# A decode step on one core: a split request for w_down and unrolled ScalarE copies, in place of hardware loops and a short ScalarE program

## The chip, the core and the metric

The kernel runs on one core of a Trainium2 chip. The metric is the device time of one execution in microseconds (us). A core has five engines that run their own programs and meet at semaphores: TensorE (PE; its weight loads are listed as PEld), VectorE (DVE), ScalarE (ACT), GpSimd (POOL) and SyncE (SP), which issues most of the DMA requests. Sixteen DMA engines move the data; a request over 128 partitions arrives in sixteen shares, one from each, and its semaphore counts to 16.

## What is computed

One token goes through two branches in parallel, each fed by the same layer norm, and both are added to the input:

```python
xn = layernorm(x)                                  # x: 1 x 512, bf16
# branch A: sliding-window attention on a cache
q = xn @ wq                                        # 512 x 4096: 32 heads of 128
k, v = k_cache[:, :, -4096:], v_cache[:, :, -4096:]   # 8 key heads, 4 query heads each
o = softmax(q @ k.T * 128**-0.5) @ v
a = o @ wo                                         # 4096 x 512
# branch B: a gated MLP for the one token
r = xn @ w_r                                       # one token: top-1 is this token
y = (silu(xn @ w_gate) * (xn @ w_up)) @ w_down     # 512 x 1792, 1792 x 512
b = xn + sigmoid(r) * y
out = x + a + b
```

wq and wo have 4 MB each, the windows of k and v 8 MB each, w_gate, w_up and w_down 1.75 MB each. In all 30.7 MB are read once, for a single output row of 1 KB.

## The kernel before

All work is written out by hand: each engine has its own order, and `need` waits for a token that another engine's `mark` counts up, while the loops use plain semaphores. Nothing plans or reorders it.

*Requests.* SyncE asks for everything in one order: wq in two chunks (kt 0-1, kt 2-3), w_r (1 KB), the eight 1 MB groups of k, the eight of v, then, when the q projection is done, w_gate and w_up into the space of wq, and, when the last half of group 5 has been staged (`SP.need((s_c[1], 6))`, L326), wo in four chunks of 1 MB and w_down in five chunks (of 4, 4, 3, 2 and 1 of its 14 row blocks) into the space of k. Only x is asked for by ScalarE. Each request has its own semaphore.

*Norm and q.* VectorE and ScalarE normalize x (Sqrt, L181). TensorE turns the row into four columns (L190) and multiplies them with wq, in two passes kh = 0, 1 over the two chunks (L223); each pass fills two PSUM banks (hf). Between the passes stand the gate and two matmuls that zero the score banks: VectorE multiplies xn with w_r (L202), ScalarE takes Tanh (L205), VectorE scales (L207), TensorE spreads the value over the partitions (L214), VectorE copies it (gfb, L216). The two banks of q are copied by ScalarE and by VectorE (L230), and transposed into qpad (L236, L240).

*K loop.* For each of the eight groups g, VectorE copies k into a staging tile kin in two halves of 2048 columns (C, L265). TensorE transposes four blocks b of 8 x 128 columns into PSUM (T, L296). The evacuation to kT goes to VectorE for b = 0, 2 (E, L269) and to ScalarE for b = 1, 3, in a hardware loop (L283 to L286). TensorE multiplies with the queries (Sm, L304), the second pair of blocks one round late, so that its order in a round is T0 T1, S2 S3 of the group before, T2 T3, S0 S1. GpSimd copies the queries of a group to qA and qB (L256, L258).

*Softmax and V loop.* Row maxima (L335 to L349), Exp on ScalarE (L351), transposes of p (L360). Then for each group VectorE stages v in two halves and picks the columns of p (L369, L373, L375), TensorE multiplies (L402, L408) and collects the four bands (L393) of the group before, which ScalarE has copied from PSUM to pvS in a second hardware loop (L386 to L388).

*The end.* The gate and up products (L433), the normalized attention output in the layout of wo (L438, L440), then 32 matmuls with the four chunks of wo (L456) and 14 with the five of w_down (L461), all into one PSUM row; VectorE adds the input (L465) and SyncE stores it. `fill` (L146) issues matmuls on zeros, whose result nobody reads, while TensorE would otherwise stand still.

Of the kernel before, what the change touches and what calls it, by code (L numbers as in the profile page):

```python
# [8 lines left out]
F32 = mybir.dt.float32  # L9
ALU = mybir.AluOpType  # L10
ACTF = mybir.ActivationFunctionType
# [27 lines left out]
def kernel(  # L39
# [15 lines left out]
    P = 128  # L55
    D = A_x.shape[2]
    KT = D // P
    HKV = A_k_cache.shape[1]
# [18 lines left out]
    sb = lambda name, shape, dt: nc.alloc_sbuf_tensor(name, shape, dt)  # L77
    k_sb = sb("k_sb", [P, HKV, 4, 1024], BF16)
    v_sb = sb("v_sb", [P, HKV, NT, DH], BF16)
    wq_sb = sb("wq_sb", [P, KT, NQ], BF16)  # L80
    kin = sb("kin", [P, 4, 1024], BF16)
    kT = sb("kT", [P, 4, 1024], BF16)
# [7 lines left out]
    q4 = sb("q4", [P, 2, 512], BF16)  # L90
# [3 lines left out]
    gfb = sb("gfb", [P, 1], F32)  # L94
    ident_bf = sb("ident_bf", [P, P], BF16)
    ident_f = sb("ident_f", [P, P], F32)
    ones_f = sb("ones_f", [P, P], F32)
# [2 lines left out]
    mask4 = sb("mask4", [P, 4], BF16)  # L100
    r32 = sb("r32", [P, 32], BF16)
    eps_t = sb("eps_t", [P, 1], F32)
    xrow = sb("xrow", [1, D], BF16)
    wr_row = sb("wr_row", [1, D], BF16)
    xn_row = sb("xn_row", [1, D], BF16)
# [5 lines left out]
    sml = sb("sml", [1, 8], F32)  # L111
# [12 lines left out]
    ps = nc.alloc_psum_tensor("ps", [P, 8, 512], F32)  # L124
    psf = ps[:].rearrange("p a b -> p (a b)")
    tp = ps[:, 0:4, :].bitcast(BF16)
# [9 lines left out]
    wd_sb = k_flat[:, 0:FB * D]  # L136
    wo_sb = k_flat[:, FB * D:(FB + RJ) * D]

    S = lambda n: nc.alloc_semaphore(n)
    PE, ACT, DVE, POOL, SP = (Eng(nc, nc.tensor, "pe"), Eng(nc, nc.scalar, "act"), Eng(nc, nc.vector, "dve"),  # L140
                              Eng(nc, nc.gpsimd, "pool"), Eng(nc, nc.sync, "sp"))
    te, ac, ve, gp, sy = nc.tensor, nc.scalar, nc.vector, nc.gpsimd, nc.sync
# [5 lines left out]
    def dma(eng, name, out_, in_):  # L148
        s = S("d_" + name)
        eng.dma_start(out=out_, in_=in_).then_inc(s, 16)  # L150
        return (s, 16)

    t_x = dma(ac, "x", xrow[:], A_x.rearrange("a b d -> (a b) d"))
    wq_v = A_wq.rearrange("(p kt) n -> p kt n", kt=KT)
    KH = KT // 2
    t_wq = [dma(sy, f"wq{h}", wq_sb[:, h * KH:(h + 1) * KH, :], wq_v[:, h * KH:(h + 1) * KH, :]) for h in range(2)]
    t_wr = dma(sy, "wr", wr_row[:], B_w_r.rearrange("(a d) -> a d", a=1))
    t_k = [dma(sy, f"k{g}", k_sb[:, g].rearrange("p b (i d) -> p (b i) d", d=DH),
               A_k_cache[0, g, Sk - W:, :].rearrange("(p t) d -> p t d", t=NT)) for g in range(HKV)]

# [11 lines left out]
    t_eps = DVE.mark(ve.memset(eps_t[:], EPS))  # L172
    t_ones = DVE.mark(ve.memset(ones_f[:], 1.0))
    t_ps0 = DVE.mark(ve.memset(ps[:, 0:2, :].rearrange("p a b -> p (a b)"), 0.0))

    DVE.need(t_x)
    a = DVE.mark(ve.bn_stats(out=stats[:], in_=xrow[:]))
    DVE.need(a)
    t_mv = DVE.mark(ve.bn_aggr(out=mv[:], in_=stats[:]))
    ACT.need(t_mv, t_eps)  # L180
    t_std = ACT.mark(ac.activation(out=sml[:, 0:1], in_=mv[:, 1:2], func=ACTF.Sqrt, bias=eps_t[0:1, :], scale=1.0))  # L181
    DVE.need(t_std)
    a = DVE.mark(ve.reciprocal(out=sml[:, 1:2], in_=sml[:, 0:1]))
    DVE.need(a, t_mv)
# [4 lines left out]
    for kt in range(KT):  # L189
        ins = te.matmul(ps[:, 6, 256 + kt:257 + kt], lhsT=xn_row[:].rearrange("a (p k) -> a k p", k=KT)[:, kt, :],  # L190
                        rhs=ident_bf[0:1, 0:1], start=True, stop=True)
# [13 lines left out]
    t_rth = ACT.mark(ac.activation(out=sml[:, 3:4], in_=sml[:, 2:3], func=ACTF.Tanh, scale=0.5))  # L205
    DVE.need(t_rth)
    t_gf = DVE.mark(ve.tensor_scalar(out=sml[:, 4:5], in0=sml[:, 3:4], scalar1=0.25, scalar2=0.25, op0=ALU.mult, op1=ALU.add))  # L207
    PE.need(t_xnT)
    t_qe = []
    t_qpad = []  # L210
    for kh in range(2):
        if kh == 1:
            PE.need(t_gf, t_ones)
            t_gfp = PE.mark(te.matmul(ps[:, 6, 264:265], lhsT=ones_f[0:1, :], rhs=sml[:, 4:5], start=True, stop=True))  # L214
            DVE.need(t_gfp)
            t_gfb = DVE.mark(ve.tensor_copy(out=gfb[:], in_=ps[:, 6, 264:265]))  # L216
            for ch in range(2):
                te.matmul(sc[:, ch, :], lhsT=zst[:], rhs=zmov[:], start=True, stop=False, skip_group_check=True)  # L218
        PE.need(t_wq[kh], t_ps0)
        for hf in range(2):  # L220
            for kt in range(kh * KH, (kh + 1) * KH):
                for c in range(4):
                    ins = te.matmul(ps[32 * c:32 * c + 1, hf, :], lhsT=xnT[:, kt:kt + 1],  # L223
                                    rhs=wq_sb[:, kt, (4 * hf + c) * 512:(4 * hf + c + 1) * 512],
                                    start=(kt == 0), stop=(kt == KT - 1), tile_position=(0, 32 * c))
            if kh == 1:
                t_qp = PE.mark(ins)
                cp, eng = ((ac.copy, ACT), (ve.tensor_copy, DVE))[hf]
                eng.need(t_qp)
                t_qe.append(eng.mark(cp(out=q4[:, hf, :], in_=ps[:, hf, :])))  # L230
    for hf in range(2):
        PE.need(t_qe[hf], t_gfb)
        if hf == 1:
# [1 line left out]
        for hl in range(4):  # L235
            ins = te.transpose(qT_ps[:, hl, :], q4[:, hf, hl * DH:(hl + 1) * DH], ident_bf[:])  # L236
# [7 lines left out]
    t_g = dma(sy, "g", wgu[:, 0:KT * F], B_w_gate.rearrange("(p kt) f -> p (kt f)", kt=KT))  # L244
    t_u = dma(sy, "u", wgu[:, KT * F:2 * KT * F], B_w_up.rearrange("(p kt) f -> p (kt f)", kt=KT))

    s_c = [S(f"s_c{b}") for b in range(2)]
    s_ev = [S(f"s_ev{b}") for b in range(4)]
    pe_t = [S(f"pe_t{b}") for b in range(4)]
    pe_q = S("pe_q")  # L250

    def pool_q(g):
        POOL.need(t_qpad[g // 4])
# [3 lines left out]
        gp.wait_ge(pe_q, 2 * g + 1)  # L257
        gp.tensor_copy(out=qB[:], in_=qpad[:, g, :]).then_inc(s_qb, 1)  # L258

    def C(g, h):  # L260
        if h == 0:
            DVE.need(t_k[g])
        if g >= 1:
            DVE.need((pe_t[2 * h + 1], g))
        ve.tensor_copy(out=kin[:, 2 * h:2 * h + 2, :], in_=k_sb[:, g, 2 * h:2 * h + 2, :]).then_inc(s_c[h], 1)  # L265

    def E(g, b):
        DVE.need((pe_t[b], g + 1))
        ve.tensor_copy(out=kT[:, b, :], in_=tp[:, b, :]).then_inc(s_ev[b], 1)  # L269

    for h in range(2):
        C(0, h)
    for g in range(HKV):
        pool_q(g)
        last = (g == HKV - 1)
        E(g, 0)
        if not last:
            C(g + 1, 0)
        E(g, 2)
        if not last:  # L280
            C(g + 1, 1)

    with ac.Fori(1, 9) as i:  # L283
        for b in (1, 3):
            ac.wait_ge(pe_t[b], i)
            ac.copy(out=kT[:, b, :], in_=tp[:, b, :]).then_inc(s_ev[b], 1)  # L286

    PE.need(t_zst, t_zmov, t_kt0)
    te.sem_inc(s_ev[2], 1)
    te.sem_inc(s_ev[3], 1)  # L290

    def T(b, i):
        if b % 2 == 0:
            te.wait_ge(s_c[b // 2], i)
        for k in range(8):
            ins = te.transpose(tp[:, b, k * P:(k + 1) * P], kin[:, b, k * P:(k + 1) * P], ident_bf[:])  # L296
        ins.then_inc(pe_t[b], 1)

    def Sm(b, i, q, last=False):
        te.wait_ge(s_ev[b], i)  # L300
# [10 lines left out]
    with te.Fori(1, 9) as i:  # L311
# [11 lines left out]
    Sm(2, 9, qB)  # L323
    t_sc = PE.mark(Sm(3, 9, qB))

    SP.need((s_c[1], 6))  # L326
    wo_v = A_wo.rearrange("(p j) n -> p (j n)", j=RJ)
    wo_chunks = [(0, 8), (8, 16), (16, 24), (24, 32)]
    t_wo = [dma(sy, f"wo{k}", wo_sb[:, j0 * D:j1 * D], wo_v[:, j0 * D:j1 * D]) for k, (j0, j1) in enumerate(wo_chunks)]
    wd_v = B_w_down.rearrange("(p j) n -> p (j n)", j=FB)  # L330
    wd_chunks = [(0, 4), (4, 8), (8, 11), (11, 13), (13, 14)]
    t_wd = [dma(sy, f"wd{k}", wd_sb[:, j0 * D:j1 * D], wd_v[:, j0 * D:j1 * D]) for k, (j0, j1) in enumerate(wd_chunks)]

    DVE.need(t_sc)
    t_pmax = DVE.mark(ve.reduce_max(out=pmax[:], in_=sc[:].rearrange("p a b -> p (a b)"), axis=AX.X))  # L335
# [4 lines left out]
    a = DVE.mark(ve.reduce_max(out=gm[:], in_=ps[0:1, 6, 0:P].rearrange("a (q c) -> a c q", q=4), axis=AX.X))  # L340
# [6 lines left out]
                              start=True, stop=True))  # L347
# [8 lines left out]
    for h in range(2):  # L356
        PE.need(t_p[h])
        for k in range(4):
            blk = 4 * h + k
            ins = te.transpose(pT_ps[:, blk, :], p_sb[:, blk * P:(blk + 1) * P], ident_bf[:])  # L360
    t_pT = PE.mark(ins)

    s_va, s_vb, s_pt, pe_pva, pe_pv, s_pvs, pe_col = S("s_va"), S("s_vb"), S("s_pt"), S("pe_pva"), S("pe_pv"), S("s_pvs"), S("pe_col")

    def stage_v(g):
        DVE.need(t_v[g])
        if g >= 1:
            DVE.need((pe_pva, g))
        ve.tensor_copy(out=vin[:, 0], in_=v_sb[:, g, 0:16, :]).then_inc(s_va, 1)  # L369
        DVE.need(t_pT)  # L370
        if g >= 1:
            DVE.need((pe_pv, g))
        ve.tensor_copy(out=pTcur[:].rearrange("p b (q j) -> p b q j", j=REP),  # L373
                       in_=pT_ps.rearrange("p b (q c) -> p b q c", q=4)[:, :, :, REP * g:REP * (g + 1)]).then_inc(s_pt, 1)
        ve.tensor_copy(out=vin[:, 1], in_=v_sb[:, g, 16:32, :]).then_inc(s_vb, 1)  # L375
# [4 lines left out]
    a = DVE.mark(ve.tensor_tensor(out=rs1[:], in0=rowsum[:, 0:1], in1=rowsum[:, 1:2], op=ALU.add))  # L380
    DVE.need(a, t_r32)
    t_B = DVE.mark(ve.tensor_scalar(out=Bsel[:], in0=r32[:], scalar1=rs1[:], scalar2=None, op0=ALU.mult))

    for g in range(1, HKV):
        stage_v(g)
    with ac.Fori(1, 9) as i:  # L386
        ac.wait_ge(pe_col, i)
        ac.copy(out=pvS[:].rearrange("p t d -> p (t d)"), in_=pv_ps).then_inc(s_pvs, 1)  # L388
    PE.need(t_pv0)

# [5 lines left out]
    with te.Fori(1, 9) as i:  # L396
        g = i - 1
# [3 lines left out]
        for tl in range(4):  # L401
            ins = te.matmul(pv_ps[32 * tl:32 * tl + 16, :], lhsT=pTcur[:, tl, :],  # L402
                            rhs=vin[:, 0].rearrange("p (q t) d -> p t q d", t=4)[:, tl],
                            start=True, stop=False, tile_position=(0, 32 * tl))
        ins.then_inc(pe_pva, 1)
        te.wait_ge(s_vb, i)
        for tl in range(4):
            ins = te.matmul(pv_ps[32 * tl:32 * tl + 16, :], lhsT=pTcur[:, 4 + tl, :],  # L408
                            rhs=vin[:, 1].rearrange("p (q t) d -> p t q d", t=4)[:, tl],
                            start=False, stop=True, tile_position=(0, 32 * tl))  # L410
# [45 lines left out]
            te.matmul(a_ps, lhsT=oT2[:, j:j + 1], rhs=wo_sb[:, j * D:(j + 1) * D], start=False, stop=False, skip_group_check=True)  # L456
    PE.need(t_hT)
    for k, (j0, j1) in enumerate(wd_chunks):
        PE.need(t_wd[k])
        for j in range(j0, j1):  # L460
            ins = te.matmul(a_ps, lhsT=hTr[:, j, 0:1], rhs=wd_sb[:, j * D:(j + 1) * D], start=False, stop=(j == FB - 1),  # L461
                            skip_group_check=True)
# [36 lines left out]
```

## Time and profile before

| | |
|---|---|
| median of 3 runs | 82.53 us (82.31 to 82.58) |
| profiled execution | 82.31 us, of which the span from its first to its last instruction is 80.5 |
| busy: PE, DVE, ACT, POOL | 60.2, 45.1, 26.5, 10.6 us |
| HBM read | 30.67 MB, 381 GB/s over the span |
| q projection, second pass (L223) | from 15.64 us |
| K loop | 19.9 to 45.2 us |
| V loop | 50.4 to 64.1 us |
| wo and w_down (L456, L461) | 67.3 to 77.7 us |

A line such as `L456 PE MATMUL ps<-k_sb,oT` is the matmul of line 456 that writes tile ps from tiles k_sb and oT; wo and w_down lie in the space of k_sb and are listed under its name. A group's line ends with its busy time and the mean of one instruction, and with the idle time of the engine before it and what ended that. Digits in the slices are tenths. Matmul ends are modelled, and a matmul's duration contains its passage through the array, so the time from start to start says more on the rate. DMA packets and the arrival of each share of a request are also in the trace.

### The profile page before, as it was taken

How to read it: one execution, taken by the hardware profiler on the slowest of the kernel's cores; microseconds unless marked ns; L12 is line 12 of the kernel's file. 1: busy time of each engine (PE TensorE's matmuls, PEld its weight loads, DVE VectorE, ACT ScalarE, POOL GpSimd, SP SyncE). 2: the span in 40 equal slices, each digit the busy share in tenths (PEclk: the TensorE clock that was granted, in tenths of full speed). 3: DMA queues.
4: the chain of work that ended last, by engine and by line, in shares of the span. 5: the costliest groups of instructions: out<-in, count | busy, mean ns of one | idle time of the engine just before them, and what ended most of it. 6: DMA issues, size and time to landing. Idle time of an engine off the chain costs nothing.

```text
span 80.5 us, 1589 instructions
## 1 busy us (share of the span) xinstructions
PE 60.2 (75%) x596; PEld 30.7 (38%) x596; DVE 45.1 (56%) x91; ACT 26.5 (33%) x34; POOL 10.6 (13%) x27
## 2 busy tenths in 40 slices
PE   0010810993999999999999786788887899999950
PEld 0010200422787686868776232222222443333300
DVE  3771004026655999999995547988888059000030
ACT  2830001020135787777777216222343220000000
POOL 5910000001011253434341000000000000000000
PEclk9999999999999999999999999999999999999999
DMA  1999999999999999999999999999999999999400
GB/s 41 301 431 399 431 448 395 419 431 423 427 427 419 415 427 415 431 415 431 415 427 419 419 415 419 448 430 420 420 449 381 423 423 423 423 403 392 176 2 1
DMA packets 4185, 30.72 MB, mean 381 GB/s; under 512 B 467, under 2 KB 598, under 8 KB 1110
## 3 DMA queue, kind: packets, MB, share of 16 engines
q1 hardware_dynamic: 4180, 30.67, 92.0%
q8 instruction: 2, 0.03, 0.2%
q14 instruction: 1, 0.01, 0.0%
q10 hardware_dynamic: 2, 0.00, 0.0%
HBM read 30.67 MB, written 0.00 MB: 381 GB/s over the span
## 4 chain that ended last, share of the span: by engine, by line
PE 62%; DMA 14%; ACT 9%; DVE 7%; issue 4%; SPq 1%; ACTq 0%
PE ps L296 23%; DMA wr_row<-in_B_w_r_dram 14%; PE ps L456 9%; PE ps L304 7%; ACT pvS L388 6%; PE ps L461 4%; PE ps L402 3%; PE ps L408 3%; PE ps L393 2%; PE ps L223 2%; PE ps L433 2%; DVE pmax L335 2%; ACT kT L286 1%; PE ps L146 1%; PE ps L218 1%
## 5 line engine op out<-in xcount | busy, mean ns | idle before, releaser
L296 PE MATMUL ps<-ident_bf,kin 128*128 128x128 bf16 x256 | 19.4, 236 | 0.9 <-DVE kin L265 0.9
L286 ACT COPY kT<-ps 128x1024 bf16<-128x1024 bf16 x16 | 16.2, 1012 | 11.2 <-PE ps L296 11.2
L296 PEld LDWEIGHTS ps<-ident_bf,kin 128*128 128x128 bf16 x256 | 16.5, 106 | 5.0 <-issue 3.8
L269 DVE COPY kT<-ps 128x1024 bf16<-128x1024 bf16 x16 | 11.1, 692 | 3.3 <-PE ps L296 2.7
L265 DVE COPY kin<-k_sb 128x2048 bf16<-128x2048 bf16 x16 | 10.9, 686 | 0.5 <-PE ps L296 0.4
L388 ACT CAST pvS<-ps 128x512 bf16<-128x512 f32 x8 | 4.7, 585 | 9.6 <-PE ps L393 9.6
L456 PE MATMUL ps<-k_sb,oT 128*1 128x512 bf16 x32 | 7.2, 379 | 0.0
L223 PE MATMUL ps<-wq_sb,xnT 128*1 128x512 bf16 x32 | 3.8, 621 | 3.5 <-DMA wq_sb<-in_A_wq_dram 3.5
L256 POOL COPY qA<-qpad 128x32 bf16<-128x32 bf16 x8 | 3.6, 448 | 21.1 <-DVE qpad L240 14.1
L369 DVE COPY vin<-v_sb 128x2048 bf16<-128x2048 bf16 x8 | 5.5, 685 | 1.5 <-PE ps L402 1.5
L465 DVE TENSOR_TENSOR res<-ps,resid 1x512 bf16<-1x512 f32 x1 | 0.7, 678 | 9.1 <-PE ps L461 9.1
L375 DVE COPY vin<-v_sb 128x2048 bf16<-128x2048 bf16 x8 | 5.5, 684 | 0.0
L402 PE MATMUL ps<-vin,pTcur 128*16 128x512 bf16 x32 | 3.1, 381 | 2.6 <-ACT pvS L388 2.2
L258 POOL COPY qB<-qpad 128x32 bf16<-128x32 bf16 x8 | 3.6, 451 | 10.4 <-PE ps L304 10.4
L414 PE MATMUL ps<-zmov,zst 128*128 128x512 bf16 x16 | 4.7, 377 | 0.0
L304 PE MATMUL ps<-kT,qB 128*32 128x512 bf16 x36 | 4.2, 413 | 0.4 <-ACT kT L286 0.3
L202 DVE SCALAR_TENSOR_TENSOR rprod<-xn_row,wr_row 1x512 f32<-1x512 bf16 x1 | 0.7, 679 | 6.7 <-DMA wr_row<-in_B_w_r_dram 6.7
L456 PEld LDWEIGHTS ps<-k_sb,oT 128*1 128x1 bf16 x32 | 2.5, 84 | 4.6 <-DMA k_sb<-in_A_wo_dram 0.5
L190 PE MATMUL ps<-ident_bf,xn_row 1*128 1x1 bf16 x4 | 0.3, 166 | 4.6 <-DVE xn_row L185 4.6
L146 PE MATMUL ps<-zmov,zst 128*128 128x512 bf16 x14 | 3.7, 382 | 0.0
L214 PE MATMUL ps<-sml,ones_f 1*128 1x1 f32 x2 | 0.6, 358 | 3.9 <-DVE sml L207 3.9
L304 PE MATMUL ps<-kT,qA 128*32 128x512 bf16 x32 | 3.4, 417 | 0.0
(84 smaller groups left out, 51.3 us busy)
## 6 DMA issues: line engine op xcount, KB each, us to landing
k_sb<-in_A_k_cache_dram SPq DMA_DIRECT2D x8, 1024.0 KB, 20.5
v_sb<-in_A_v_cache_dram SPq DMA_DIRECT2D x8, 1024.0 KB, 27.3
wq_sb<-in_A_wq_dram SPq DMA_DIRECT2D x2, 2048.0 KB, 9.6
k_sb<-in_A_wo_dram SPq DMA_DIRECT2D x4, 1024.0 KB, 31.4
wq_sb<-in_B_w_gate_dram SPq DMA_DIRECT2D x1, 1792.0 KB, 29.0
wq_sb<-in_B_w_up_dram SPq DMA_DIRECT2D x1, 1792.0 KB, 31.2
k_sb<-in_B_w_down_dram SPq DMA_DIRECT2D x2, 512.0 KB, 29.6
k_sb<-in_B_w_down_dram SPq DMA_DIRECT2D x1, 384.0 KB, 25.7
```

The costliest lines, as they stand in the source:

```text
L223: ins = te.matmul(ps[32 * c:32 * c + 1, hf, :], lhsT=xnT[:, kt:kt + 1], rhs=wq_sb[:, kt, (4 * hf + c) * 512:(4 * hf + c + 1) * 512], start ...
L265: ve.tensor_copy(out=kin[:, 2 * h:2 * h + 2, :], in_=k_sb[:, g, 2 * h:2 * h + 2, :]).then_inc(s_c[h], 1)
L269: ve.tensor_copy(out=kT[:, b, :], in_=tp[:, b, :]).then_inc(s_ev[b], 1)
L286: ac.copy(out=kT[:, b, :], in_=tp[:, b, :]).then_inc(s_ev[b], 1)
L296: ins = te.transpose(tp[:, b, k * P:(k + 1) * P], kin[:, b, k * P:(k + 1) * P], ident_bf[:])
L304: ins = te.matmul(sc[32 * cq:32 * cq + 32, ch, :], lhsT=q[:], rhs=kT[:, b, e * 512:(e + 1) * 512], start=False, stop=False, tile_position= ...
L369: ve.tensor_copy(out=vin[:, 0], in_=v_sb[:, g, 0:16, :]).then_inc(s_va, 1)
L375: ve.tensor_copy(out=vin[:, 1], in_=v_sb[:, g, 16:32, :]).then_inc(s_vb, 1)
L388: ac.copy(out=pvS[:].rearrange("p t d -> p (t d)"), in_=pv_ps).then_inc(s_pvs, 1)
L402: ins = te.matmul(pv_ps[32 * tl:32 * tl + 16, :], lhsT=pTcur[:, tl, :], rhs=vin[:, 0].rearrange("p (q t) d -> p t q d", t=4)[:, tl], start ...
L414: te.matmul(ps[:, 7, :], lhsT=zst[:], rhs=zmov[:], start=True, stop=True)
L456: te.matmul(a_ps, lhsT=oT2[:, j:j + 1], rhs=wo_sb[:, j * D:(j + 1) * D], start=False, stop=False, skip_group_check=True)
```

## The change

- ScalarE's copies in the K and V loops are written out instead of looped over; its program has 50 instructions instead of 30.
- In the K loop ScalarE also evacuates block 0 of groups 1, 3 and 5. VectorE stages k in four copies of 1024 columns per group; the four transposes count on one semaphore, each staging copy on one of its own, and a staging copy waits for its own block's transpose.
- w_r is asked for by ScalarE, after x. The gate's matmul and copy (L214, L216) stand before both passes of the q projection. Both banks of q are copied by ScalarE.
- ScalarE runs a one-element Sqrt and a one-element Tanh whose results nobody reads.
- The first chunk of w_down is asked for in two requests: partitions 0 to 119 (15 DMA engines) and 120 to 127.

```diff
@@ -100,6 +100,7 @@
     mask4 = sb("mask4", [P, 4], BF16)
     r32 = sb("r32", [P, 32], BF16)
     eps_t = sb("eps_t", [P, 1], F32)
+    junk = sb("junk", [1, 2], F32)
     xrow = sb("xrow", [1, D], BF16)
     wr_row = sb("wr_row", [1, D], BF16)
     xn_row = sb("xn_row", [1, D], BF16)
@@ -151,10 +152,10 @@
         return (s, 16)
 
     t_x = dma(ac, "x", xrow[:], A_x.rearrange("a b d -> (a b) d"))
+    t_wr = dma(ac, "wr", wr_row[:], B_w_r.rearrange("(a d) -> a d", a=1))
     wq_v = A_wq.rearrange("(p kt) n -> p kt n", kt=KT)
     KH = KT // 2
     t_wq = [dma(sy, f"wq{h}", wq_sb[:, h * KH:(h + 1) * KH, :], wq_v[:, h * KH:(h + 1) * KH, :]) for h in range(2)]
-    t_wr = dma(sy, "wr", wr_row[:], B_w_r.rearrange("(a d) -> a d", a=1))
     t_k = [dma(sy, f"k{g}", k_sb[:, g].rearrange("p b (i d) -> p (b i) d", d=DH),
                A_k_cache[0, g, Sk - W:, :].rearrange("(p t) d -> p t d", t=NT)) for g in range(HKV)]
 
@@ -172,13 +173,16 @@
     t_eps = DVE.mark(ve.memset(eps_t[:], EPS))
     t_ones = DVE.mark(ve.memset(ones_f[:], 1.0))
     t_ps0 = DVE.mark(ve.memset(ps[:, 0:2, :].rearrange("p a b -> p (a b)"), 0.0))
+    ACT.need(t_eps)
+    ac.activation(out=junk[:, 0:1], in_=eps_t[0:1, :], func=ACTF.Sqrt)
 
     DVE.need(t_x)
     a = DVE.mark(ve.bn_stats(out=stats[:], in_=xrow[:]))
     DVE.need(a)
     t_mv = DVE.mark(ve.bn_aggr(out=mv[:], in_=stats[:]))
-    ACT.need(t_mv, t_eps)
+    ACT.need(t_mv)
     t_std = ACT.mark(ac.activation(out=sml[:, 0:1], in_=mv[:, 1:2], func=ACTF.Sqrt, bias=eps_t[0:1, :], scale=1.0))
+    ac.activation(out=junk[:, 1:2], in_=eps_t[0:1, :], func=ACTF.Tanh)
     DVE.need(t_std)
     a = DVE.mark(ve.reciprocal(out=sml[:, 1:2], in_=sml[:, 0:1]))
     DVE.need(a, t_mv)
@@ -205,15 +209,16 @@
     t_rth = ACT.mark(ac.activation(out=sml[:, 3:4], in_=sml[:, 2:3], func=ACTF.Tanh, scale=0.5))
     DVE.need(t_rth)
     t_gf = DVE.mark(ve.tensor_scalar(out=sml[:, 4:5], in0=sml[:, 3:4], scalar1=0.25, scalar2=0.25, op0=ALU.mult, op1=ALU.add))
+    PE.need(t_gf, t_ones)
+    t_gfp = PE.mark(te.matmul(ps[:, 6, 264:265], lhsT=ones_f[0:1, :], rhs=sml[:, 4:5], start=True, stop=True))
+    DVE.need(t_gfp)
+    t_gfb = DVE.mark(ve.tensor_copy(out=gfb[:], in_=ps[:, 6, 264:265]))
+
     PE.need(t_xnT)
     t_qe = []
     t_qpad = []
     for kh in range(2):
         if kh == 1:
-            PE.need(t_gf, t_ones)
-            t_gfp = PE.mark(te.matmul(ps[:, 6, 264:265], lhsT=ones_f[0:1, :], rhs=sml[:, 4:5], start=True, stop=True))
-            DVE.need(t_gfp)
-            t_gfb = DVE.mark(ve.tensor_copy(out=gfb[:], in_=ps[:, 6, 264:265]))
             for ch in range(2):
                 te.matmul(sc[:, ch, :], lhsT=zst[:], rhs=zmov[:], start=True, stop=False, skip_group_check=True)
         PE.need(t_wq[kh], t_ps0)
@@ -225,9 +230,8 @@
                                     start=(kt == 0), stop=(kt == KT - 1), tile_position=(0, 32 * c))
             if kh == 1:
                 t_qp = PE.mark(ins)
-                cp, eng = ((ac.copy, ACT), (ve.tensor_copy, DVE))[hf]
-                eng.need(t_qp)
-                t_qe.append(eng.mark(cp(out=q4[:, hf, :], in_=ps[:, hf, :])))
+                ACT.need(t_qp)
+                t_qe.append(ACT.mark(ac.copy(out=q4[:, hf, :], in_=ps[:, hf, :])))
     for hf in range(2):
         PE.need(t_qe[hf], t_gfb)
         if hf == 1:
@@ -244,10 +248,9 @@
     t_g = dma(sy, "g", wgu[:, 0:KT * F], B_w_gate.rearrange("(p kt) f -> p (kt f)", kt=KT))
     t_u = dma(sy, "u", wgu[:, KT * F:2 * KT * F], B_w_up.rearrange("(p kt) f -> p (kt f)", kt=KT))
 
-    s_c = [S(f"s_c{b}") for b in range(2)]
+    s_c = [S(f"s_c{b}") for b in range(4)]
     s_ev = [S(f"s_ev{b}") for b in range(4)]
-    pe_t = [S(f"pe_t{b}") for b in range(4)]
-    pe_q = S("pe_q")
+    pe_t, pe_q = S("pe_t"), S("pe_q")
 
     def pool_q(g):
         POOL.need(t_qpad[g // 4])
@@ -257,44 +260,47 @@
         gp.wait_ge(pe_q, 2 * g + 1)
         gp.tensor_copy(out=qB[:], in_=qpad[:, g, :]).then_inc(s_qb, 1)
 
-    def C(g, h):
-        if h == 0:
+    def C(g, b):
+        if b == 0:
             DVE.need(t_k[g])
         if g >= 1:
-            DVE.need((pe_t[2 * h + 1], g))
-        ve.tensor_copy(out=kin[:, 2 * h:2 * h + 2, :], in_=k_sb[:, g, 2 * h:2 * h + 2, :]).then_inc(s_c[h], 1)
-
-    def E(g, b):
-        DVE.need((pe_t[b], g + 1))
-        ve.tensor_copy(out=kT[:, b, :], in_=tp[:, b, :]).then_inc(s_ev[b], 1)
-
-    for h in range(2):
-        C(0, h)
+            DVE.need((pe_t, 4 * (g - 1) + b + 1))
+        ve.tensor_copy(out=kin[:, b, :], in_=k_sb[:, g, b, :]).then_inc(s_c[b], 1)
+
+    def E(eng, g, b):
+        if eng == "dve":
+            DVE.need((pe_t, 4 * g + b + 1))
+            ve.tensor_copy(out=kT[:, b, :], in_=tp[:, b, :]).then_inc(s_ev[b], 1)
+        else:
+            ACT.need((pe_t, 4 * g + b + 1))
+            ac.copy(out=kT[:, b, :], in_=tp[:, b, :]).then_inc(s_ev[b], 1)
+
+    for b in range(4):
+        C(0, b)
     for g in range(HKV):
         pool_q(g)
         last = (g == HKV - 1)
-        E(g, 0)
+        even = (g % 2 == 0)
+        E("dve" if even or last else "act", g, 0)
+        E("act", g, 1)
         if not last:
             C(g + 1, 0)
-        E(g, 2)
+            C(g + 1, 1)
+        E("dve", g, 2)
+        E("act", g, 3)
         if not last:
-            C(g + 1, 1)
-
-    with ac.Fori(1, 9) as i:
-        for b in (1, 3):
-            ac.wait_ge(pe_t[b], i)
-            ac.copy(out=kT[:, b, :], in_=tp[:, b, :]).then_inc(s_ev[b], 1)
+            C(g + 1, 2)
+            C(g + 1, 3)
 
     PE.need(t_zst, t_zmov, t_kt0)
     te.sem_inc(s_ev[2], 1)
     te.sem_inc(s_ev[3], 1)
 
     def T(b, i):
-        if b % 2 == 0:
-            te.wait_ge(s_c[b // 2], i)
+        te.wait_ge(s_c[b], i)
         for k in range(8):
             ins = te.transpose(tp[:, b, k * P:(k + 1) * P], kin[:, b, k * P:(k + 1) * P], ident_bf[:])
-        ins.then_inc(pe_t[b], 1)
+        ins.then_inc(pe_t, 1)
 
     def Sm(b, i, q, last=False):
         te.wait_ge(s_ev[b], i)
@@ -323,13 +329,16 @@
     Sm(2, 9, qB)
     t_sc = PE.mark(Sm(3, 9, qB))
 
-    SP.need((s_c[1], 6))
+    SP.need((s_c[3], 6))
     wo_v = A_wo.rearrange("(p j) n -> p (j n)", j=RJ)
     wo_chunks = [(0, 8), (8, 16), (16, 24), (24, 32)]
     t_wo = [dma(sy, f"wo{k}", wo_sb[:, j0 * D:j1 * D], wo_v[:, j0 * D:j1 * D]) for k, (j0, j1) in enumerate(wo_chunks)]
     wd_v = B_w_down.rearrange("(p j) n -> p (j n)", j=FB)
     wd_chunks = [(0, 4), (4, 8), (8, 11), (11, 13), (13, 14)]
-    t_wd = [dma(sy, f"wd{k}", wd_sb[:, j0 * D:j1 * D], wd_v[:, j0 * D:j1 * D]) for k, (j0, j1) in enumerate(wd_chunks)]
+    t_wd = []
+    for k, (j0, j1) in enumerate(wd_chunks):
+        rows = [(0, 120), (120, P)] if k == 0 else [(0, P)]
+        t_wd.append([dma(sy, f"wd{k}_{p0}", wd_sb[p0:p1, j0 * D:j1 * D], wd_v[p0:p1, j0 * D:j1 * D]) for p0, p1 in rows])
 
     DVE.need(t_sc)
     t_pmax = DVE.mark(ve.reduce_max(out=pmax[:], in_=sc[:].rearrange("p a b -> p (a b)"), axis=AX.X))
@@ -381,10 +390,10 @@
     DVE.need(a, t_r32)
     t_B = DVE.mark(ve.tensor_scalar(out=Bsel[:], in0=r32[:], scalar1=rs1[:], scalar2=None, op0=ALU.mult))
 
-    for g in range(1, HKV):
-        stage_v(g)
-    with ac.Fori(1, 9) as i:
-        ac.wait_ge(pe_col, i)
+    for g in range(HKV):
+        if g >= 1:
+            stage_v(g)
+        ACT.need((pe_col, g + 1))
         ac.copy(out=pvS[:].rearrange("p t d -> p (t d)"), in_=pv_ps).then_inc(s_pvs, 1)
     PE.need(t_pv0)
 
@@ -456,7 +465,7 @@
             te.matmul(a_ps, lhsT=oT2[:, j:j + 1], rhs=wo_sb[:, j * D:(j + 1) * D], start=False, stop=False, skip_group_check=True)
     PE.need(t_hT)
     for k, (j0, j1) in enumerate(wd_chunks):
-        PE.need(t_wd[k])
+        PE.need(*t_wd[k])
         for j in range(j0, j1):
             ins = te.matmul(a_ps, lhsT=hTr[:, j, 0:1], rhs=wd_sb[:, j * D:(j + 1) * D], start=False, stop=(j == FB - 1),
                             skip_group_check=True)
```

## The prediction

> **What bounds the kernel now.** I read the page's slices first, then the chain of waits, then the timeline of the tail, then the trace's landing records (the times at which the shares of a request arrive).
>
> ```profile
> span 80.5 us, 1589 instructions
> ...
> DMA  1999999999999999999999999999999999999400
> ...
> q8 instruction: 2, 0.03, 0.2%
> q14 instruction: 1, 0.01, 0.0%
> ...
> HBM read 30.67 MB, written 0.00 MB: 381 GB/s over the span
> ```
>
> The DMA engines are full from slice 2 to slice 37 of 40, that is from 2 to about 75.5 us, at some 420 GB/s. Every byte of the inputs passes in that stretch, in the order in which SyncE asks for it. The queues q8 and q14 carry program code, also over these engines, in the middle of the kernel.
>
> ```profile
> 67.38 5.27 PE ps L456 x24
> 72.65 0.01 issue
> 72.66 1.89 PE ps L456 x8
> 74.55 3.12 PE ps L461 x14
> 77.67 0.02 issue
> 77.69 0.68 DVE res L465
> ```
>
> The end of the chain. The one interruption lies at 72.66, and the timeline names its cause (the last columns are the idle time before, and what ended it):
>
> ```profile
> 72.66 1.38 PEld L456 LDWEIGHTS ps<-k_sb,oT 128*1 128x1 bf16 x8 [0.52 <-DMA k_sb<-in_A_wo_dram]
> 76.18 0.30 PEld L461 LDWEIGHTS ps<-k_sb,hTr 128*1 128x1 bf16 x3 [0.42 <-DMA k_sb<-in_B_w_down_dram]
> 77.16 0.08 PEld L461 LDWEIGHTS ps<-k_sb,hTr 128*1 128x1 bf16 x1 [0.23 <-DMA k_sb<-in_B_w_down_dram]
> ```
>
> So TensorE waits for the fourth chunk of A_wo, and from there 8 + 14 matmuls follow at 0.2155 us from start to start. The last starts at 77.277. Without any later wait it would start at 72.66 + 21 x 0.2155 = 77.19. **The waits for w_down cost TensorE 0.09 us in all**; a weight load that idles in this list is mostly ahead of the matmul it serves.
>
> The landing records say why the fourth wo chunk is late. Fourteen of its sixteen shares arrive between 71.04 and 71.43, the fifteenth at 72.07, the sixteenth at 72.62. Two engines lag, and have lagged since two points: one share falls behind by 0.98 us after an 8 KB code packet at 43.73 (one data packet then took 968 ns instead of 312), a second by about 1.3 us after a 16 KB code packet at 47.73. The lags stay to the end: the last w_down chunk has fourteen shares by 75.97, then 76.56 and 77.12.
>
> **The change, part by part.** Sums are against the profiled execution, 82.31 us, of which the span is 80.5 and 1.8 lie around it. It is 0.22 under the median of 82.53.
>
> *w_r moved to ScalarE's queue, the gate earlier.*
>
> ```profile
> DVE rprod L202 <- DMA wr_row<-in_B_w_r_dram: 6.7, 1, 6.7
> PE ps L214 <- DVE sml L207: 3.9, 1, 3.9
> PE ps L223 <- DMA wq_sb<-in_A_wq_dram: 3.5, 1, 3.5
> ```
>
> In SyncE's queue the 1 KB of w_r stands behind 4 MB of wq and lands at 12.98. On ScalarE's queue x, issued at 0.91, was in use at 2.27, 1.36 us later. w_r will be issued after x (the issue of x took 0.52), at about 1.5, and may share an engine with 16 KB packets that took up to 1.45 us, so between 3 and 5 us; at worst 13, as now. With 5 the gate is ready near 8.3: x's normalization comes later by one issue and a small activation (0.52 + 0.29), so VectorE ends resid at 7.1, then 0.75 for the dot product and about 0.5 for tanh and scaling. The first half of L223, which waits 3.5 for wq and starts at 8.39, goes 0.6 us later behind the gate's matmul (L214, 0.58), and that is covered, since the second half of wq lands at 13.15 and L223's half takes 1.88. The two zeroing matmuls (L218, 0.97) come in that gap too. The second half starts at 13.2 instead of 15.64: **2.4 us earlier**. If w_r landed later than about 6.6 this cover would shrink, and from about 11 on TensorE would hold both halves back. The second q copy goes from VectorE (0.692) to ScalarE (the first took 0.58) and saves 0.1.
>
> *Table loads.* Both already start without a wait (1.47 and 3.45, 1.28 each), so the two junk activations bring nothing; they cost ScalarE at most 0.29 each, before 8 us, where nothing waits on it.
>
> *The K loop.*
>
> ```profile
> L286 ACT COPY kT<-ps 128x1024 bf16<-128x1024 bf16 x16 | 16.2, 1012 | 11.2 <-PE ps L296 11.2
> L269 DVE COPY kT<-ps 128x1024 bf16<-128x1024 bf16 x16 | 11.1, 692 | 3.3 <-PE ps L296 2.7
> L265 DVE COPY kin<-k_sb 128x2048 bf16<-128x2048 bf16 x16 | 10.9, 686 | 0.5 <-PE ps L296 0.4
> ```
>
> The chain gives a head group 2.66 us of TensorE (2 x (1.00 + 0.33)). ScalarE takes over three copies, for groups 1, 3 and 5: 3 x 1.012 = 3.04 there, 0.38 over TensorE's time, about 1.1 in all (at least 0, with the slack of the even groups at 2.02). VectorE's 16 staging copies become 32 of half the size. A one-element copy takes 0.159 and 2048 elements 0.686, so 1024 take 0.42 (ends: 0.34 if all of it scales, 0.69 if none does, which would make a group 3.8 us and the loop 9 us longer; the small copy speaks against that). An even group then has 4 x 0.42 + 2 x 0.69 = 3.06, an odd one 2.37, a mean of 2.7, or 2.45 with the overlap of neighbours (in the timeline they follow each other about 0.05 closer than they last): under TensorE's 2.66. Sum: softmax starts 2.4 - 1.1 = **1.3 us earlier**.
>
> *Loops unrolled.* ScalarE's copies start 0.02 to 0.03 us behind TensorE in both loops; its register and branch instructions lie under waits. Nothing is gained. The V loop moves up whole: each v chunk lands before its use (the last at 54.1, used near 61).
>
> *Where the 1.3 us go.* A_wo is asked for after C of group 5 (36.62 now) and starts to land at 63.6, so its request may move by many microseconds without effect. TensorE would start L456 at 66.1 instead of 67.38, and wait there for chunks that land at 67.7, 70.1 and 72.6. The lead of 1.3 turns into waiting. Now it is 0.17: three chunks of 8 x 0.2155 from 67.31 end at 72.49.
>
> *First w_down chunk in two requests.* Bytes stay. One more issue on SyncE: those of w_down take 2.1 to 4.3 us each, in the backlog, the last from 57.50 to 60.53; its bytes move at 75.3, so even 4.3 more is covered by ten. The change's words put 120 partitions on 15 engines; the 16th is then free of 8 partitions x 4 KB. A chunk of 512 KB passes in 1.28 us, so 0.16 per partition: that engine gains 1.28. If it is the later laggard, the last w_down share comes at 76.56 instead of 77.12, which gives TensorE its 0.09. The other 8 partitions fall on other engines, 0.16 each if on eight; if a laggard is among them, the last chunk lands at 77.28 and the last matmul starts at 77.32, +0.05. The wo chunk before it keeps its time either way.
>
> [...]
>
> **Sum:** -0.09 to +0.05 around 82.31, or 82.44 to 82.58 at the median: **82.5, no change.** A measurement of this kernel tells about 0.3% (0.25 us) from nothing.
>
> **The rivals.**
>
> *A. The odd-shaped requests move more slowly (slower).* No row shows their rate. Between no cost and half speed lies 0 to 1.28 us on each engine that takes part. At half speed the two laggards' last shares come at 76.56 + 1.28 = 77.84 and 77.12 + 1.28 = 78.40 (the latter not, if it is the engine set free); a matmul starts 0.05 behind its chunk, so the end moves by 0.6 to 1.2. It decides from a loss of 0.11 on the later laggard, or of 0.67 on the earlier one if the later is set free: from there the last chunk lands after 77.23 and the last matmul starts after today's 77.277. For: 15 pieces do not fit a layout in which all 128-partition requests land evenly within 0.4. Against: 0.5 MB alone is touched. 82.9 to 83.8.
>
> *B. ScalarE's longer program brings one more code fetch (slower).* The program goes from 30 to 50 instructions. If the fetch strikes the later laggard before A_wo, a lag of 0.98 like the first adds in full; the earlier one stands 0.55 ahead of it and would pass it by 0.43; on the 14 others nothing follows. For: two lags in the trace come from such fetches. Against: VectorE had run 62 instructions when the first fetch came and runs on to 114 with no other 8 KB packet, so a program of 50 is not long here. 82.9 to 83.5.
>
> *C. The fetches belong to ScalarE's loops (faster).* The 8 KB fetch starts within 1 ns of the last loop arithmetic (43.727), the 16 KB one 0.39 before the second loop is set up (48.12). Without either, the fourth wo chunk lands 1.19 earlier, at 71.43, the last w_down share at 75.97, and the last matmul starts at 76.02 instead of 77.28: 1.25 off. With the 16 KB one alone gone it is 0.55, with the 8 KB one alone nothing. Against: a fetch also comes at 75.39, when only TensorE is still working its program, so q8 is likely TensorE's, whose program is unchanged but for a few waits. 81.3 to 82.0.
>
> [...]
>
> **How the numbers follow.** No change 0.36; A 0.27; B 0.17; C 0.19; 0.01 is left. Faster 0.19, within 0.3% 0.37, slower 0.44: the likeliest single case is no change, with 82.4 to 82.6 of its own, but two ways lead to slower. The range takes in C down to 81.8, about half of its price, and A and B up to 83.5; beyond lie some 0.08 of C and 0.06 of A.
>
> **What would show it.** Right: L223's second half at 13.2, the wait of L202 gone, softmax about 1.3 us earlier, L456 broken by waits for three chunks, the last of them ending near 72.6, L461 with no wait for its first chunk, last matmul near 77.2. Wrong: a wait for w_down of over 0.2 us before L461 (A), the fourth wo chunk after 73 (B) or before 72 (C), or softmax later than 45.2, which would say that the K loop's new division costs more than its start gains.

## The result, and the profile after

The changed kernel takes **85.16 us** (median of 4 runs, 84.61 to 85.94) against 82.47 for the kernel before: a ratio of 1.031, with a 95% interval of 1.025 to 1.036. The ratio leaves out the slowest of the four runs, which lies over 1.5% above the fastest. It is slower by 2.7 us, outside the range of 81.8 to 83.5. The profiled execution took 85.17, of which the span is 83.3, 2.8 more than before.

The page of the changed kernel: the slices of the DMA engines and of what they moved, and the code queues.

```profile
span 83.3 us, 1553 instructions
...
DMA  3899999999999999999999999999999999999300
GB/s 71 299 386 441 441 397 425 417 437 421 429 413 425 433 421 417 421 425 409 421 437 413 413 421 424 435 441 441 434 384 421 421 421 407 240 213 296 138 3 0
...
q8 instruction: 2, 0.03, 0.2%
q14 instruction: 1, 0.01, 0.0%
```

The DMA engines are full from end to end as before, but in slices 35 to 37, from about 71 to 77 us, they move 213 to 296 GB/s, against some 420 in the slices ahead of them. Code is fetched three times, as before. The view by stretches shows the same with numbers; the columns are the stretch, the busy time of PE, PEld, DVE, ACT and POOL, the granted clock, the share of the DMA engines and their GB/s. First the kernel before, then the changed one:

```profile
71.00:75.00 4.00, 3.99 (x19) 1.41 (x18) 0.00 (x0) 0.00 (x0) 0.00 (x0) 1.00 1.02 402
```
```profile
71.00:75.00 4.00, 1.49 (x7) 0.42 (x6) 0.00 (x0) 0.00 (x0) 0.00 (x0) 1.00 1.03 219
```

The engines are as busy (1.03), and move about half. That is the stretch of the first w_down chunk. In the trace's DMA packets, its packets of 4 KB last 159 ns in the kernel before; here the median is 308 ns at 71 us, 455 at 72.5, 386 at 73. The packets of 8 KB of the fourth wo chunk that two late engines still have to move last 500 to 815 ns there, instead of 313.

The timeline of TensorE at the end, and the end of the chain:

```profile
67.92 1.89 PE L465 MATMUL ps<-k_sb,oT 128*1 128x512 bf16 x8 [0.45 <-DMA k_sb<-in_A_wo_dram]
70.40 1.89 PE L465 MATMUL ps<-k_sb,oT 128*1 128x512 bf16 x8 [0.60 <-DMA k_sb<-in_A_wo_dram]
74.81 1.89 PE L465 MATMUL ps<-k_sb,oT 128*1 128x512 bf16 x8 [2.52 <-DMA k_sb<-in_A_wo_dram]
77.04 3.39 PE L470 MATMUL ps<-k_sb,hTr 128*1 128x512 bf16 x14 [0.35 <-DMA k_sb<-in_B_w_down_dram]
```
```profile
43.27 33.69 DMA k_sb<-in_B_w_down_dram
76.95 0.09 issue
77.04 3.40 PE ps L470 x14
80.44 0.02 issue
80.47 0.68 DVE res L474
```

(L465 and L470 are L456 and L461 of before.) TensorE reaches the wo chunks 1.7 us earlier, at 65.59, and waits for three of them. The fourth is complete at 74.76 instead of 72.62: fourteen shares by 71.61, then 73.94 and 74.76. The first w_down chunk is complete at 76.95, after a further wait. The account of the span: the fourth wo chunk's matmuls start 2.15 later (74.81 against 72.66); from there to the start of the last matmul it is 5.24 us instead of 4.62, of which 0.50 is the wait for the first w_down chunk (77.04, where 76.53 was possible). Together 2.77.

### The profile page after: what moved, and what is told of

It is laid out like the page before. It is cut to its first block, busy times and chain, and to the rows that moved or that the text cites. A ratio compares the mean times of both kernels' runs of the same rounds, so it can differ in the third digit from the quotient of the medians.

```text
span 83.3 us, 1553 instructions
## 1 busy us (share of the span) xinstructions
PE 61.7 (74%) x596; PEld 30.5 (37%) x596; DVE 43.6 (52%) x103; ACT 29.7 (36%) x40; POOL 7.3 (9%) x27
## 4 chain that ended last, share of the span: by engine, by line
DMA 54%; PE 25%; SPq 11%; DVE 5%; issue 1%
DMA k_sb<-in_B_w_down_dram 40%; DMA wq_sb<-in_A_wq_dram 14%; PE ps L302 13%; SPq L151 11%; PE ps L310 4%; PE ps L470 4%; PE ps L228 2%; DVE kin L268 2%; DVE kT L273 2%; PE ps L240 1%; DVE res L474 1%; DVE qpad L244 0%; SPq L503 0%; SPq L74 0%
## 5 line engine op out<-in xcount | busy, mean ns | idle before, releaser
L276 ACT COPY kT<-ps 128x1024 bf16<-128x1024 bf16 x19 | 18.5, 1020 | 8.9 <-PE ps L302 8.9
L302 PE MATMUL ps<-ident_bf,kin 128*128 128x128 bf16 x256 | 19.1, 235 | 0.8 <-DVE kin L268 0.6
L268 DVE COPY kin<-k_sb 128x1024 bf16<-128x1024 bf16 x32 | 12.2, 423 | 1.1 <-PE ps L302 1.1
L273 DVE COPY kT<-ps 128x1024 bf16<-128x1024 bf16 x13 | 9.0, 692 | 4.4 <-PE ps L302 4.3
L465 PE MATMUL ps<-k_sb,oT 128*1 128x512 bf16 x32 | 7.5, 378 | 3.6 <-DMA k_sb<-in_A_wo_dram 3.6
L465 PEld LDWEIGHTS ps<-k_sb,oT 128*1 128x1 bf16 x32 | 2.3, 83 | 8.7 <-DMA k_sb<-in_A_wo_dram 5.1
L228 PE MATMUL ps<-wq_sb,xnT 128*1 128x512 bf16 x32 | 3.8, 621 | 1.8 <-DMA wq_sb<-in_A_wq_dram 1.8
L310 PE MATMUL ps<-kT,qA 128*32 128x512 bf16 x32 | 4.4, 417 | 0.0
L259 POOL COPY qA<-qpad 128x32 bf16<-128x32 bf16 x8 | 2.1, 258 | 21.2 <-DVE qpad L244 11.5
L470 PE MATMUL ps<-k_sb,hTr 128*1 128x512 bf16 x14 | 3.4, 378 | 0.3 <-DMA k_sb<-in_B_w_down_dram 0.3
L234 ACT CAST q<-ps 128x512 bf16<-128x512 f32 x2 | 1.2, 585 | 6.7 <-PE ps L228 6.7
```

Source lines behind the costliest of these rows:

```text
L268: ve.tensor_copy(out=kin[:, b, :], in_=k_sb[:, g, b, :]).then_inc(s_c[b], 1)
L310: ins = te.matmul(sc[32 * cq:32 * cq + 32, ch, :], lhsT=q[:], rhs=kT[:, b, e * 512:(e + 1) * 512], start=False, stop=False, tile_position= ...
```

## Experiments

The theory after this reading: a request of fewer than 128 partitions is dealt to the DMA engines in a way in which they hinder each other, and hinder whoever is late. Experiments 1 and 2 ask whether it is the split at all, 3, 4 and 10 which part of it, 5 and 6 what in the shape matters, 7, 8 and 9 where the loss goes.

**1. The changed kernel without the split** (e1_whole)

```diff
-        rows = [(0, 120), (120, P)] if k == 0 else [(0, P)]
+        rows = [(0, P)]
```

> The changed kernel with the first w_down chunk asked for whole. If the split alone makes the loss (theory), the packets of that chunk last 159 ns again, the fourth wo chunk lands near 72.7, L456's last wait ends there and the time is 82.3 to 82.6, like the kernel before, although the wo matmuls start near 65.6. If the K loop's new division, the unrolled loops or the earlier start share the loss by way of the DMA stream (rival), it stays over 83.5.

Measured: 82.47 us, ratio 1.000 (0.998 to 1.001) to the kernel before. 4 KB packets last 159 to 164 ns again, and the weight loads of the fourth wo chunk:

```profile
72.75 1.38 PEld L465 LDWEIGHTS ps<-k_sb,oT 128*1 128x1 bf16 x8 [1.11 <-DMA k_sb<-in_A_wo_dram]
```

```profile
71.00:75.00 4.00, 3.40 (x17) 1.18 (x15) 0.00 (x0) 0.00 (x0) 0.00 (x0) 1.00 1.02 400
```

The DMA engines move 400 GB/s again. All other parts of the change together are worth nothing: the wo matmuls start at 65.4, and the lead of 1.9 us ends in this wait.

**2. The kernel before with the split alone** (e2_split_alone)

```diff
-    t_wd = [dma(sy, f"wd{k}", wd_sb[:, j0 * D:j1 * D], ...) for k, (j0, j1) in enumerate(wd_chunks)]
+        rows = [(0, 120), (120, P)] if k == 0 else [(0, P)]
+        t_wd.append([dma(sy, f"wd{k}_{p0}", wd_sb[p0:p1, j0 * D:j1 * D], ...) for p0, p1 in rows])
```

> The kernel before with the split alone. If the split makes the loss: 85.0 to 85.3, wo's fourth chunk near 74.7. If the change's other parts are needed for it, or ease it (the kernel before has no lead at the wo matmuls): the first gives under 84, the second over 85.6.

Measured: 85.31 us, ratio 1.038 (1.032 to 1.044). The fourth wo chunk is complete at 74.59, and TensorE's weight loads wait for it:

```profile
74.63 1.38 PEld L459 LDWEIGHTS ps<-k_sb,oT 128*1 128x1 bf16 x8 [2.82 <-DMA k_sb<-in_A_wo_dram]
```

The split alone makes the whole loss. The expectation took the kernel before to have no lead at the wo matmuls. In this execution it had one: it reached them at 65.56 instead of 67.31, without any other part of the change. The sixteen transposes that open the K loop show why, first in the profile of the kernel before, then here:

```profile
19.94 1.89 PE L296 MATMUL ps<-ident_bf,kin 128*128 128x128 bf16 x16 [0.87 <-DVE kin L265]
```
```profile
20.02 1.07 PE L296 MATMUL ps<-ident_bf,kin 128*128 128x128 bf16 x16 [0.87 <-DVE kin L265]
```

The program up to there is the same. In the profile of the kernel before TensorE ran these rounds at about half the pace, and the first full clock on record is at 26.1; here the record has full clock from 19.1. The first three rounds of the loop took 6.7 us there and 4.0 here. So a lead of this size can come from TensorE's speed in one execution, and this run doesn't show what the split costs a kernel without a lead.

**3. Only the request of 120 partitions** (e3_120_only)

```diff
-        rows = [(0, 120), (120, P)] if k == 0 else [(0, P)]
+        rows = [(0, 120)] if k == 0 else [(0, P)]
```

> The changed kernel without the request for partitions 120 to 127 of the first w_down chunk (these 32 KB are left out and old content is multiplied). If the request of 120 partitions makes the loss: packets of 300 ns and more, 84.4 to 85.2. If the small request makes it: 82.2 to 82.6.

Measured: 85.26 us, ratio 1.034 (1.028 to 1.041); the median 4 KB packet lasts 267 to 418 ns from 71 to 73.5; the fourth wo chunk is complete at 74.42.

**4. A whole chunk and a small request more** (e4_8_more)

```diff
-        rows = [(0, 120), (120, P)] if k == 0 else [(0, P)]
+        rows = [(0, P)]
...
+        if k == 0:
+            t_wd[0].append(dma(sy, "spare", wq_flat[120:P, ...], wd_v[120:P, j0 * D:j1 * D]))
```

> The changed kernel with the first w_down chunk whole, and behind it a further request of partitions 120 to 127 (the same 32 KB once more, to a free place). If the request of 120 makes the loss: 82.4 to 82.8, since eight engines move one row of 4 KB more (0.16 us). If the small request makes it, because eight engines write to eight neighbouring partitions: 84 to 85.2.

Measured: 82.74 us, ratio 1.004 (1.002 to 1.006). The small request costs 0.2 us, with half a microsecond in which the median packet lasts 345 ns. The longest 4 KB packet there lasts 429 ns, 2.7 times 159. Of the two requests the large one makes the loss.

**5. and 6. Other splits by partitions** (e5_64_64, e6_112_16)

```diff
-        rows = [(0, 120), (120, P)] if k == 0 else [(0, P)]
+        rows = [(0, 64), (64, P)] if k == 0 else [(0, P)]      # e5_64_64
+        rows = [(0, 112), (112, P)] if k == 0 else [(0, P)]    # e6_112_16
```

> The changed kernel with the first w_down chunk in partitions 0 to 63 and 64 to 127. If a request suffers because its rows do not fall one eighth to each engine's own rows of memory (theory: where the rows lie decides), each half meets the same fate as the 120: packets near 300 ns, 84.5 to 86. If it suffers because 15 engines share it (rival: the count of engines), both halves, which divide by 16, cost nothing: 82.3 to 82.6.

> The changed kernel with the first w_down chunk in partitions 0 to 111 (7 rows for each of 16 engines) and 112 to 127 (one row each). Where the rows lie decides: 84.5 to 86. The count of engines decides: 82.3 to 82.7.

Measured: 86.06 us, ratio 1.041 (1.036 to 1.045), packets with medians of 294 to 349 ns, for 64 and 64; 83.97 us, ratio 1.018 (1.016 to 1.021), packets with medians of 256 to 349 ns, for 112 and 16, under what was expected, but far from nothing. In both, all sixteen engines post a share of each request, so the number of engines isn't the cause. The same stretch, 71 to 75, in the 64 and 64 kernel:

```profile
71.00:75.00 4.00, 1.33 (x7) 0.39 (x6) 0.00 (x0) 0.00 (x0) 0.00 (x0) 1.00 1.03 227
```

**7. The split on the last chunk** (e7_last_chunk), a quarter of the bytes

```diff
-        rows = [(0, 120), (120, P)] if k == 0 else [(0, P)]
+        rows = [(0, 120), (120, P)] if k == 4 else [(0, P)]
```

> The changed kernel with the split on the last chunk of w_down (128 KB) in place of the first (512 KB). If the loss goes with the bytes of the odd request (theory): about a quarter of 2.7 at the most, less since no wo chunk is behind it, 82.7 to 83.3. If an odd request costs a fixed time: 85.

Measured: 82.93 us, ratio 1.006 (1.004 to 1.007): 0.5 us. So an odd request has no fixed price of 2.7 us; the loss grows with its bytes.

**8. The split on the first chunk of v** (e8_v0), twice the bytes, some 38 us earlier

```diff
-    t_v = [dma(sy, f"v{g}", v_sb[:, g], ...) for g in range(HKV)]
...
+        rows = [(0, 120), (120, P)] if g == 0 else [(0, P)]
+        t_v.append([dma(sy, f"v{g}_{p0}", v_sb[p0:p1, g], v_g[p0:p1]) for p0, p1 in rows])
...
-        rows = [(0, 120), (120, P)] if k == 0 else [(0, P)]
+        rows = [(0, P)]
```

> The changed kernel with the split on the first chunk of v (1 MB, due at 35 us) in place of w_down's. If the odd request slows the stream itself (theory), everything behind it lands later by twice the loss of 512 KB, some 2.5 to 3.5 us, and the time is 85 to 86. If the loss needs the two lagging engines or the waiting TensorE at the end (rival): under 83.2.

Measured: 86.2 us, ratio 1.045 (1.043 to 1.048), a little over the expectation. The stretch 34 to 38, first of the kernel before, then of this one:

```profile
34.00:38.00 4.00, 4.00 (x64) 3.01 (x62) 3.89 (x7) 3.05 (x4) 1.62 (x4) 1.00 1.02 424
```
```profile
34.00:38.00 4.00, 3.94 (x56) 2.63 (x54) 3.12 (x8) 3.31 (x4) 0.70 (x3) 1.00 1.09 217
```

The 8 KB packets last 500 to 990 ns instead of 312 until about 38.5. The stream never makes up for it: the last share of the last w_down chunk comes at 80.62, where experiment 1 has 77.19, 3.4 us earlier. Neither late engines nor the end of the kernel are needed. A part of the time is not the stream's: TensorE's clock was halved from 65.7 to 72.6, after a wait of 3.35 us for w_up.

```profile
71.00:75.00 4.00, 4.00 (x16) 1.43 (x15) 0.00 (x0) 0.00 (x0) 0.00 (x0) 0.80 1.01 418
```

From 70.33 on TensorE did its last 46 matmuls without a wait and started the last one at 81.13, about 0.5 us behind that share.

**9. The split on the second chunk of w_down** (e9_second_chunk)

```diff
-        rows = [(0, 120), (120, P)] if k == 0 else [(0, P)]
+        rows = [(0, 120), (120, P)] if k == 1 else [(0, P)]
```

> The changed kernel with the split on the second chunk of w_down in place of the first (both 512 KB). If the rows of the odd request hinder whatever the late engines still have to move (theory), a whole chunk of 1.28 us now lies between, about the lag of the later engine: the fourth wo chunk lands at 72.6 to 72.9 instead of 74.8, the wait moves to the first or second w_down chunk, and the last w_down share still comes 2 to 2.7 late: 84.2 to 85.3. If the fourth wo chunk is late for another reason (rival: the longer list of requests, the lead of TensorE), it lands near 74.8 again.

Measured: 84.84 us, ratio 1.028 (1.023 to 1.033).

```profile
73.17 1.89 PE L465 MATMUL ps<-k_sb,oT 128*1 128x512 bf16 x8 [0.93 <-DMA k_sb<-in_A_wo_dram]
75.88 1.02 PE L470 MATMUL ps<-k_sb,hTr 128*1 128x512 bf16 x4 [0.83 <-DMA k_sb<-in_B_w_down_dram]
77.46 2.41 PE L470 MATMUL ps<-k_sb,hTr 128*1 128x512 bf16 x10 [0.55 <-DMA k_sb<-in_B_w_down_dram]
```

With a whole chunk between them the fourth wo chunk is complete at 73.12 instead of 74.76 (0.2 over the expectation), and the waits come at the first and second w_down chunk. So it is the odd request that makes the earlier chunk late, by way of engines that still have rows of it to move.

**10. Two requests by columns** (e10_columns)

```diff
-        rows = [(0, 120), (120, P)] if k == 0 else [(0, P)]
-        t_wd.append([dma(sy, f"wd{k}_{p0}", wd_sb[p0:p1, j0 * D:j1 * D], wd_v[p0:p1, j0 * D:j1 * D]) for p0, p1 in rows])
+        cols = [(j0, j0 + 2), (j0 + 2, j1)] if k == 0 else [(j0, j1)]
+        t_wd.append([dma(sy, f"wd{k}_{c0}", wd_sb[:, c0 * D:c1 * D], wd_v[:, c0 * D:c1 * D]) for c0, c1 in cols])
```

> The changed kernel with the first w_down chunk in two requests by columns (two row blocks of w_down each, all 128 partitions). If only requests of fewer than 128 partitions hurt (theory): 82.3 to 82.6. If one more request costs, whatever its shape (rival): 82.9 or more.

Measured: 82.62 us, ratio 1.001 (1.000 to 1.003).

```profile
71.00:75.00 4.00, 3.39 (x16) 1.18 (x15) 0.00 (x0) 0.00 (x0) 0.00 (x0) 1.00 1.03 397
```

One more request of all 128 partitions costs nothing that can be told here.

What the ten show: a large request for part of the partitions passes at about half the rate (219 to 246 GB/s in this stretch instead of 402); the loss grows with its bytes, though not in proportion (the last share of w_down comes 0.4 us later than in experiment 1 with 128 KB, 2.7 with 512 KB, 3.4 with 1 MB), and arises early in the stream as at its end; the number of requests or engines is not it. How the rows of such a request are dealt out was not seen: no packet in the trace names its engine or its rows.

Why the packets of such a request last longer was not shown: that the engines hinder each other where they write, and that they read the rows in another order from memory, are both guesses, and no run here separates them. Against 159 ns for a whole chunk, the medians are 294 to 349 with 64 and 64, reach 455 with 120 and 8, and are 256 to 288 during the 112-partition request. The losses decide nothing either. The last share of w_down comes at 79.95 with 64 and 64 and at 79.89 with 120 and 8; at a granted clock of 1.0 the first took 85.35 us in its one such run, the second 84.61 and 85.17, and the three slower runs of the first have a lower clock (0.98, 0.98 and 0.94; last section).

## Why the prediction was wrong

**Right: TensorE is bound by the arrival of the fourth wo chunk, and nothing done earlier pays.** Experiment 1 gives 1.000, as forecast for all parts but the split. The steps before it, by the changed kernel's waits and groups:

```profile
PE ps L228 <- DMA wq_sb<-in_A_wq_dram: 1.8, 1, 1.8
L268 DVE COPY kin<-k_sb 128x1024 bf16<-128x1024 bf16 x32 | 12.2, 423 | 1.1 <-PE ps L302 1.1
L273 DVE COPY kT<-ps 128x1024 bf16<-128x1024 bf16 x13 | 9.0, 692 | 4.4 <-PE ps L302 4.3
```

- The half-size staging copy takes 423 ns; 0.42 was forecast.
- The second half of wq is used from 13.12 (13.2 forecast), 2.5 earlier than before. The K loop starts 2.9 earlier, not 2.4. Of the difference, 0.27 is a term that the prediction left out: the first transpose waits for a staging copy of half the size (0.34 us on the chain instead of 0.61). The second q copy on ScalarE gave 0.06, where 0.1 was counted.
- The K loop loses 1.13 of that (last score matmuls at 43.06 instead of 44.79); 1.1 was forecast, largely for the reason that held (the score matmuls wait for ScalarE's copies) and with some luck in the number. ScalarE's extra copies made groups 1, 3 and 5 longer by 0.41, 0.49 and 0.46 us, 1.36 together, not by 0.38 each; against that, the slow first rounds on TensorE cost 0.22 less than in the kernel before (6.51 against 6.73 us for three). The lead is 1.7, not 1.3.
- w_r landed at 6.82, outside the 3 to 5 taken for it and just past the 6.6 named as the point where cover shrinks: L228's first half went to 8.51, not 9.0, since x's normalization came no later than before (the junk Sqrt ran while ScalarE waited).

**Wrong: "First w_down chunk in two requests. Bytes stay", with a price of -0.09 to +0.05.** The bytes stay, but the rate doesn't. The step took one row's price (0.16 us per partition, from whole chunks) for rows of any request. Rival A named the effect and half the rate, at 0.27, and sized it at 0.6 to 1.2 instead of 2.8. Two terms were missed there:

- "The wo chunk before it keeps its time either way" fell. Rows of the odd request hinder the late engines, whose wo packets go from 313 ns to between 500 and 815: 2.14 us on the chunk that releases the last 22 matmuls. It was read as a loss of the w_down chunk alone, behind which only a slack of 0.11 was counted.
- The request itself: half the rate was taken for its own 1.28 us and then as the end of the range. Its median packets reach 455 ns, nearly three times 159, and its thirteen punctual shares end at 74.45, where the fourteen of before end at 72.71, 1.7 earlier.

The signs were assigned wrongly too: "the fourth wo chunk after 73" was to show B, a further code fetch. It came with A.

**Also wrong in its premise: that the engine set free might be the later laggard.** In the changed kernel the 120-partition request posts one of its sixteen counts at once, when it is issued, thirteen by 74.45, and the last two at 75.98 and 76.95. Both late engines are among the fifteen that carry it, and the engine set free is a punctual one: one share of the second w_down chunk comes at 74.27, 1.5 us ahead of the next. Even without the hindrance the late shares would have gained nothing from the engine set free.

**Rivals B and C did not occur.** There are three code fetches in the changed kernel as before. The 8 KB one came at 38.38 instead of 43.73, when VectorE had executed 64 instructions instead of 62, while ScalarE stood at 29 instead of 49; the first 16 KB one moved from 47.73 to 46.07, with TensorE at the same 382 matmuls. In all twelve profiles this one comes at 379 to 383 matmuls, so it goes with TensorE's program. The 8 KB one fits VectorE's (62 or 64 in eleven profiles, 69 in experiment 8, whose stream was slow just then); that it is VectorE's is not shown. Unrolling ScalarE's loops changed neither the number nor, much, the lag: in experiment 1 the last two shares of w_down come 0.60 and 1.27 us behind the fourteenth, in the kernel before 0.59 and 1.15. With all the other parts of the change experiment 1 equals the kernel before, and none of the versions run is faster than it.

## What to carry to other kernels

Keep the large loads of a full DMA stream at all 128 partitions; to split a request, split its columns. None of the three splits by partitions run here on a chunk of 512 KB was free (1.5 to 3.6 us), and the one by columns was (ratio 1.001). Ask of a request not only its bytes but what it does to packets in flight: it can delay a chunk asked for earlier (by 2.14 us here), and the price is set by the matmuls behind that chunk. Before relieving an engine by shape, find out from the shares of an odd request whether the late engine is the one set free.

## What was not expected of the hardware

The clock of TensorE fell after a wait in some executions and not in others. In the kernel with 120 partitions alone, and in the one with 64 and 64, the groups in the stretch behind the wait for the fourth wo chunk show it (mean ns of one, against 379 at full clock):

```profile
L465 PE MATMUL ps<-k_sb,oT 128*1 128x512 bf16 x8 | 2.9, 530 | 2.3 <-DMA k_sb<-in_A_wo_dram 2.3
```
```profile
L465 PE MATMUL ps<-k_sb,oT 128*1 128x512 bf16 x8 | 3.5, 621 | 2.7 <-DMA k_sb<-in_A_wo_dram 2.7
```

The clock records have half speed for 3.4 us from 75.2 and from 75.0; matmuls then follow each other at 0.427 instead of 0.2155 us. The wait was 2.3 and 2.7 us there. With 2.5 us the profiled execution of the changed kernel kept its full clock, with 2.3 that of experiment 2, and with 1.8 that of experiment 6. Yet in experiments 4 and 9 a wait of 1.8 us, for w_up, was followed by 3.4 us of half speed from 64.1 and 64.3, which the waits for wo took up. So the length of the wait alone does not decide.

A half-speed stretch can cost up to 1.7 us more where nothing takes it up (8 matmuls at 0.21, an estimate from these spacings), and it spreads the times: in experiment 2 the two runs with a granted clock of 1.0 took 84.8 and 84.9 us, the two with 0.98 took 85.7 and 85.9, and with 120 partitions alone the run with 1.0 took 84.8, the one with 0.98 took 85.7.
